# First expert's gating on ScalarE instead of GpSimd, early second x sums, one store a tile, and a new order for the last pair, in an attention and routed-experts kernel

## The chip, the cores and the metric

The kernel runs on one core of one Trainium2 chip. Its time is the device time of one execution, in microseconds (us); the number that counts is the median of three runs. TensorE is called PE, VectorE DVE, ScalarE ACT, GpSimd POOL and SyncE SP, as the profile has them.

## The reference

Two computations follow each other. The first is a linear attention over q, k and v of [8 batches, 8 heads, 576 positions, 64 features]; its result, written as one row for each batch and position, is `x` of [4608, 512]. The second sends every row through eight experts, each a two-layer network, and adds them up with weights that eight rounds of balancing make:

```
phi(t) = concat(relu(t) * cos(theta), relu(t) * sin(theta))
kv  = phi(k)^T v            z = sum over positions of phi(k)
x   = (phi(q) kv) / (phi(q) z + 1e-6)
P   = exp(x @ w_gate - max)                       # [4608, 8]
8 times:  P /= row sums;  P /= column sums;  P *= 4608/8
out = sum over e of P[:, e] * (relu(x @ w1[e]) @ w2[e])
```

`w1[e]` is [512, 1024] and `w2[e]` [1024, 512]. Inputs and output are f32; the kernel multiplies in f16 and adds in f32.

## The kernel before

**Layout.** Rows of `x` are counted in an order of the kernel's own: position p*9+c of batch b is row p of chunk w = 9b+c, 64 rows a chunk. A tile `g` is 128 rows, chunks 2g and 2g+1, so there are 36 tiles. `acc(g)` is the f32 output tile of 128x512 in SBUF (`acc_lo` for the first 32, `acc_hi` for the last four), and `xT` holds `x` transposed in f16.

**Phase 1, to about 230 us.** Attention of one batch after the other is interleaved by a table of slots with expert 0's two layers, in nine blocks of 512 rows. Expert 0's result goes into `acc` without its weight, for the weights are not known yet. Beside the last two blocks run the first steps of the balancing (`balanced`), and the first `x_sums`. In this phase PE, DVE and ACT are reached through `te`, `ve` and `se`, wrappers (`InOrder`) that bind each engine to the written order of instructions. Where `ve` or `se` is set back to the engine itself, a scheduler orders the instructions: in the kernel before, ACT is free from the start of phase 2 and DVE after the first unit of expert 1.

**Phase 2, experts 1 to 7.** Each expert runs six units `n` of 2x384 rows (one half from the first half of the rows and one from the second), about 18.3 us a unit. Both layers use a scheme with seven products in place of eight for a 2x2 block multiplication, which needs sums of inputs beforehand.
- `x_sums` makes three sums of `x` for a unit (S1, S2, S4) and overwrites one part of `xT`, four DVE instructions in all, and saves the three sums in DRAM by three SP transfers; `x_again` loads them back for the later experts. The tiles have two buffers.
- `group` is the first layer of 128 hidden features and their partners: seven products of two matmuls with 384 columns. It uses three PSUM banks, X (`h_ps`), Y (`copied_ps`) and Z (`p7_ps`). ACT copies X to Y (L712), takes the snapshots u2 and u4 (L699) and the two relus of Y and X (L722, L731); DVE closes the two others (`add_relu`, L693). X is written by four products in a row, each after ACT has read the one before.
- After each product of `group` stands a `fill()`. From the second unit on, `pair_fill` puts one step of the second layer there, three times out of four.
- `Pair` is the second layer of one unit's third: two tiles g1 and g2, in seven steps P1, P2, P7, P6, P4, P5, P3 of four matmuls with 256 columns. U and V are the halves of one of three PSUM banks (`rows`), W half a bank more; ACT copies U to W after P1 (L790), DVE makes four sums of the hidden features (`sums`, L774, f16), and DVE adds to `acc` with the expert's weight (`add`, L760). In the very last pair, `sums` runs on POOL, and is written ahead of the steps that are left after the last group. The order of all steps is a list sorted by `OFFSETS` (`OFFSETS_LAST` for the last pair).
- `gate(n)` (L901) multiplies the six expert-0 tiles of unit n by P[:, 0] on POOL, 36 instructions in place, after each unit of expert 1 is written and before its pairs add to those tiles.
- `store` (L163 to L170) writes a finished tile to DRAM by two transfers of 64 rows, both on SP; for the last pair the second one goes through ACT.

POOL also issues the loads of the next expert's weights (L118, L124), written after the gates.

Of the kernel before, what the change touches and what calls it, by code (L numbers as in the profile page):

```python
# [14 lines left out]
ALU = mybir.AluOpType  # L15
# [10 lines left out]
def kernel(  # L26
# [26 lines left out]
    assert KT == HK and N % TCH == 0  # L53
# [109 lines left out]
    def store(g, both=False):  # L163
        for half in range(2):
            w_ = 2 * g + half
            b, c = w_ // C, w_ % C
            rows = out[b * S : (b + 1) * S].rearrange("(p c) d -> p c d", c=C)
            (nc.scalar if half and both else nc.sync).dma_start(
                out=rows[:, c, :], in_=acc(g)[half * HP : (half + 1) * HP, :]
            )  # L170

# [417 lines left out]
    se = nc.scalar  # L589
# [107 lines left out]
    def snapshot(ps, name):  # L697
        t = u_pool.tile([P, TU], F16, name=name)
        nc.scalar.copy(out=t[:], in_=ps[:, 0:TU])  # L699
        return t  # L700
# [3 lines left out]
    def group(hT, tw, xs, n, i, fill):  # L704

        b11, T1, b21, b22, T2, T3, T4 = tw
        s1, s2, s4 = (t[:] for t in xs)
        h11, h12 = hT[:, i, 0:TU], hT[:, FH + i, 0:TU]
        h21, h22 = hT[:, i, TU : 2 * TU], hT[:, FH + i, TU : 2 * TU]
        X = ps_h[0].tile([P, TCH], FP32, name="h_ps")  # L710
        product(X, b11, x_part(0, 0, n), True)
        nc.scalar.copy(out=Y[:, 0:TU], in_=X[:, 0:TU])  # L712
        fill()
        for fn in late:
            fn()
        late.clear()
        fill()
        product(X, T2, s2, False)
        u2 = snapshot(X, "u2")
        fill()  # L720
        product(Y, b21, x_part(0, 1, n), False)
        nc.scalar.activation(out=h11, in_=Y[:, 0:TU], func=AF.Relu)  # L722
        fill()
        product(X, T1, s1, False)
        u4 = snapshot(X, "u4")
        fill()
        product(Z, T3, x_part(1, 0, n), True)
        add_relu(h22, Z, u4)
        fill()
        product(X, b22, s4, False)  # L730
        nc.scalar.activation(out=h12, in_=X[:, 0:TU], func=AF.Relu)  # L731
        fill()

        def last():
            product(Z, T4, x_part(1, 1, n), False)
            add_relu(h21, Z, u2)

        late.append(last)


    class Pair:
        def __init__(self, k, hT, e, w, c1, g1, c2, g2, first, last):
# [5 lines left out]
            self.U, self.V = self.rows[:, 0:DH], self.rows[:, DH : 2 * DH]  # L748
            self.W = W2[:, k % 2 * DH : (k % 2 + 1) * DH]
# [8 lines left out]
        def add(self, g, rows, a=None):  # L758
            a = acc(g) if a is None else a
            ve.scalar_tensor_tensor(  # L760
                out=a, in0=rows, scalar=P_tok[:, g, self.e : self.e + 1], in1=a,
                op0=ALU.mult, op1=ALU.add,
            )

        def sums(self):
# [3 lines left out]
            for out_, in0, in1, op in (  # L769
                (S1[:], self.a21, self.a22, ALU.add), (S2[:], S1[:], self.a11, ALU.subtract),  # L770
                (self.a21, self.a11, self.a21, ALU.subtract),
                (S4[:], self.a12, S2[:], ALU.subtract),
            ):
                (nc.gpsimd if self.last else ve).tensor_tensor(  # L774
                    out=out_, in0=in0, in1=in1, op=op
                )
            self.S1, self.S2, self.S4 = S1[:], S2[:], S4[:]

        def step(self, name):
# [3 lines left out]
            if name == "P1":  # L783
# [6 lines left out]
                nc.scalar.copy(out=self.W, in_=self.U)  # L790
                if not self.last:
                    self.sums()
            elif name == "P7":
# [4 lines left out]
                self.mult(self.V, self.a21, tw2[1])  # L798
            elif name == "P6":
                self.mult(self.U, self.S2, tw2[0])  # L800
                self.add(self.g2, self.rows)
            elif name == "P2":
                self.mult(self.W, self.a12, b21)
                self.add(self.g1, self.W, acc(self.g1)[:, 0:DH])
            elif name == "P4":
                self.mult(self.V, self.a22, tw2[2])
                if self.last:
                    self.add(self.g2, self.V, acc(self.g2)[:, 0:DH])
                    store(self.g2, True)
# [9 lines left out]
            elif name == "P3":  # L819
                self.mult(self.U, self.S4, b22)  # L820
                self.add(self.g1, self.U, acc(self.g1)[:, DH:Dm])
                if self.e == E - 1:
                    store(self.g1, self.last)
# [73 lines left out]
    def gate(n):  # L897

        for pair in of_unit(n):
            for g in pair[::-1]:  # L900
                nc.gpsimd.tensor_scalar(  # L901
                    out=acc(g), in0=acc(g), scalar1=P_tok[:, g, 0:1], scalar2=None, op0=ALU.mult,
                )
# [8 lines left out]
    xs_next = x_tiles()  # L912
    sums_x = x_sums(0, xs_next)
    for j in range(B - 1, NJ):
        hT = next_h()
        tiles = halves(hT, w0, [(ts * P, j * TCH // P + ts) for ts in range(TCH // P)])
        for slot in range(NS):
# [8 lines left out]
            if j == B - 1 and slot:  # L926
                next(sums_x, None)
            since = (j - B + 1) * NS + slot - 5
# [8 lines left out]
    OFFSETS_LAST = {"P1": 0, "P7": 4, "P6": 5, "P2": 7, "P5": 8, "P4": 9, "P3": 10}  # L937
    stream = []
    slot2 = -2
    n_pairs = 0  # L940

    def add_pairs(hT, e, w, n):
        nonlocal n_pairs
        for i, (g1, g2) in enumerate(of_unit(n)):
            last = e == E - 1 and n == NU - 1 and i == UG - 1
            pair = Pair(n_pairs, hT, e, w, i * P, g1, TU + i * P, g2, n == 0 and i == 0, last)
            for name, offset in (OFFSETS_LAST if last else OFFSETS).items():
# [15 lines left out]
    def pair_fill():  # L963
        nonlocal k_fill, slot2
        k_fill += 1
        if k_fill % 4 and stream and stream[0][0] <= slot2:
            _, pair, name = stream.pop(0)
            pair.step(name)
        slot2 += bool(k_fill % 4)

    mark(Y[:])
    for e in range(1, E):
        w = w_next
        for n in range(NU):
            hT = next_h()
            xs = xs_next
            for i in range(FH):
                group(hT, tws[i], xs, n, i, start_fill if e == 1 and n == 0 else pair_fill)
                m = (n + 1) % NU
                if e == 1 and m:  # L980

                    if i == 0:
# [17 lines left out]
            if e == 1 and n == 0:  # L1000
# [6 lines left out]
                w2_first(w)  # L1007
                ve = nc.vector
            if e == 1:
                gate(n)  # L1010
# [8 lines left out]

    stream[-1][1].sums()  # L1020
    while stream:
        _, pair, name = stream.pop(0)
        pair.step(name)
# [28 lines left out]
```

The softmax here doesn't subtract the row's maximum and nothing guards it: scores larger than these inputs give would overflow.

## Time and profile before

| | |
|---|---|
| three runs | 1012.5, 1012.6, 1011.53 us; median 1012.5 |
| the profiled execution's own time | 1011.92 us |
| its span, first to last instruction | 1010.2 us |
| mean granted clock of PE | 0.994 |
| the 36 gates on POOL | 226.7 to 287.4 us, shortest 1.55 us, median 1.57 |
| units of expert 1 (start of the first product) | 231.8, 251.8, 271, 290.5, 308.7 us |
| last unit's second layer begins, span ends | 988.5, 1010.2 us |
| first and last store issued by SP | 906.9, 1006.6 us |
| PE busy in 230 to 327, in 327 to 897, in 897 to 1010.2 | 92.8 of 97, 568.6 of 570, 104.7 of 113.2 us |

The page is one execution. Its first lines give the busy time of each engine, as microseconds, share of the span, and instructions. The slices cut the span in 40 (25.3 us each), with the busy tenths of each engine, one digit a slice. A group line reads: line, engine, operation, output and inputs with shapes, count, then busy microseconds and mean nanoseconds of one, then the idle time just before them and what ended it. A window line gives, for a stretch, its length, then the busy time (and count) of PE, of PE's weight loads, of DVE, ACT and POOL, then the granted clock, the busy share of the 16 DMA engines, and GB/s. A waits line gives who waited for what, and total microseconds, times and the longest. A timeline line gives start, duration, engine, line, operation and tiles, and in brackets the idle time before it and what ended it.

### The profile page before, as it was taken

How to read it: one execution, taken by the hardware profiler on the slowest of the kernel's cores; microseconds unless marked ns; L12 is line 12 of the kernel's file. 1: busy time of each engine (PE TensorE's matmuls, PEld its weight loads, DVE VectorE, ACT ScalarE, POOL GpSimd, SP SyncE). 2: the span in 40 equal slices, each digit the busy share in tenths (PEclk: the TensorE clock that was granted, in tenths of full speed). 3: DMA queues.
4: the chain of work that ended last, by engine and by line, in shares of the span. 5: the costliest groups of instructions: out<-in, count | busy, mean ns of one | idle time of the engine just before them, and what ended most of it. 6: DMA issues, size and time to landing. Idle time of an engine off the chain costs nothing.

```text
span 1010.2 us, 20651 instructions
## 1 busy us (share of the span) xinstructions
PE 983.8 (97%) x8062; PEld 690.7 (68%) x8062; DVE 840.3 (83%) x1861; ACT 556.5 (55%) x1250; POOL 117.3 (12%) x116
## 2 busy tenths in 40 slices
PE   7999999998999999999999999999999999999996
PEld 6555555445677777777777777777777777777775
DVE  5888777689999888888879888988789888987876
ACT  5766666355555555555555555555555555555551
POOL 6312200009930000000000000000000000000001
PEclk8999999999999999999999999999999999999998
DMA  9966510531302331044013310133103401114434
GB/s 168 201 91 86 88 20 1 107 58 41 81 24 50 64 67 47 25 80 76 25 48 66 65 49 25 36 78 66 49 24 67 89 25 33 39 33 127 113 87 113
DMA packets 51762, 66.50 MB, mean 66 GB/s; under 512 B 4816, under 2 KB 43472, under 8 KB 51664
## 3 DMA queue, kind: packets, MB, share of 16 engines
q0 software_dynamic: 27232, 30.94, 19.8%
q1 hardware_dynamic: 24272, 33.98, 12.4%
q8 instruction: 63, 1.03, 0.4%
q14 instruction: 35, 0.29, 0.1%
q10 hardware_dynamic: 160, 0.26, 0.1%
HBM read 83.12 MB, written 12.98 MB: 95 GB/s over the span
## 4 chain that ended last, share of the span: by engine, by line
PE 88%; DVE 9%; DMA 1%; issue 1%; ACT 1%; POOL 0%; DVEq 0%; POOLq 0%; ACTq 0%
PE rows_ps L100 32%; PE h_ps L100 25%; PE p_ps L100 10%; PE copied_ps L100 10%; PE y_ps L100 5%; PE small_ps L100 4%; DVE H L693 1%; DVE k_p L100 1%; DVE acc_lo L760 1%; DMA k_ld<-in_k_dram 1%; DVE q_pT L100 1%; DVE acc_hi L760 1%; DVE q_p L100 0%; DMA q_ld<-in_q_dram 0%; DVE den L100 0%
## 5 line engine op out<-in xcount | busy, mean ns | idle before, releaser
L760 DVE SCALAR_TENSOR_TENSOR acc_lo<-rows_ps,P_tok,acc_lo 128x512 f32<-128x512 f32 (+1 forms) x322 | 205.0, 640 | 75.1 <-PE rows_ps L100 75.1
L100 PEld LDWEIGHTS <-H 128*128 128x128 f16 x2080 | 203.5, 98 | 85.6 <-DVE H L774 2.3
L100 PEld LDWEIGHTS <-w1e 128*128 128x128 f16 x1632 | 155.8, 98 | 58.3 <-issue 3.6
L100 PE MATMUL h_ps<-xT,w1e 128*128 128x384 f16 (+1 forms) x616 | 152.9, 350 | 0.0
L731 ACT ACTIVATE H<-h_ps 128x384 f16<-128x384 f32 x168 | 82.5, 491 | 112.0 <-PE h_ps L100 112.0
L712 ACT COPY copied_ps<-h_ps 128x384 f32<-128x384 f32 x168 | 78.7, 468 | 41.2 <-PE h_ps L100 40.3
L722 ACT ACTIVATE H<-copied_ps 128x384 f16<-128x384 f32 x168 | 82.7, 492 | 23.5 <-PE copied_ps L100 23.5
L100 PE MATMUL rows_ps<-w2e,H 128*128 128x256 f16 (+1 forms) x568 | 91.7, 286 | 0.0
L100 PE MATMUL copied_ps<-xT,w1e 128*128 128x384 f16 x336 | 82.1, 326 | 0.0
L100 PE MATMUL copied_ps<-w2e,H 128*128 128x256 f16 x504 | 75.6, 273 | 0.0
L118 POOL DMA_DIRECT2D w1e<-in_moe_w_dram x11 | 8.3, 770 | 455.2 <-DVE T_3_10517 L671 83.4
L760 DVE SCALAR_TENSOR_TENSOR acc_lo<-copied_ps,P_tok,acc_lo 128x256 f32<-128x256 f32 x126 | 60.1, 477 | 0.5
L760 DVE SCALAR_TENSOR_TENSOR acc_hi<-rows_ps,P_tok,acc_hi 128x512 f32<-128x512 f32 (+1 forms) x57 | 42.0, 736 | 20.5 <-PE rows_ps L100 20.3
L790 ACT COPY copied_ps<-rows_ps 128x256 f32<-128x256 f32 x126 | 45.0, 357 | 23.3 <-PE rows_ps L100 23.0
L901 POOL TENSOR_SCALAR acc_lo<-acc_lo,P_tok 128x512 f32<-128x512 f32 x32 | 53.2, 1678 | 16.7 <-DVE P_tok L100 16.6
L100 PE MATMUL y_ps<-w2e,hT 128*128 128x512 f16 x224 | 54.7, 380 | 0.0
L774 DVE TENSOR_TENSOR H<-H 128x512 f16<-128x512 f16 x125 | 54.1, 433 | 0.0
L100 ACT ACTIVATE hT<-h_ps 128x512 f16<-128x512 f32 x54 | 32.3, 600 | 17.0 <-PE h_ps L100 16.6
L100 DVE TENSOR_TENSOR xT<-small_ps,rb 128x384 f16<-128x384 f32 x64 | 26.2, 451 | 16.6 <-ACT rb L100 16.5
L100 PEld LDWEIGHTS <-hT 128*128 128x128 f16 x224 | 19.5, 98 | 25.0 <-issue 5.8
L100 ACT COPY rb<-small_ps 128x384 f32<-128x384 f32 x64 | 22.4, 402 | 22.7 <-PE small_ps L100 22.6
L100 DVE TENSOR_SCALAR q_pT<-small_ps 128x384 f16<-128x384 f32 x46 | 25.0, 553 | 9.3 <-PE small_ps L100 8.8
(2450 smaller groups left out, 2036.3 us busy)
## 6 DMA issues: line engine op xcount, KB each, us to landing
out_dram<-acc_lo SPq DMA_DIRECT2D x63, 128.0 KB, 2.4
w1e<-in_moe_w_dram POOLq DMA_DIRECT2D x7, 1024.0 KB, 9.0
w2e<-in_moe_w_dram POOLq DMA_DIRECT2D x7, 1024.0 KB, 9.3
k_ld<-in_k_dram POOLq DMA_DIRECT2D x16, 288.0 KB, 6.3
v_ld<-in_v_dram POOLq DMA_DIRECT2D x16, 288.0 KB, 6.9
q_ld<-in_q_dram POOLq DMA_DIRECT2D x16, 288.0 KB, 6.4
w1e<-in_moe_w_dram POOLq DMA_DIRECT2D x4, 256.0 KB, 10.5
w2e<-in_moe_w_dram POOLq DMA_DIRECT2D x4, 256.0 KB, 10.8
```

The costliest lines, as they stand in the source:

```text
L100: i = getattr(self.engine, name)(*args, **kwargs)
L118: nc.gpsimd.dma_start(out=w[0][:, :, f0:f1], in_=view[:, :, f0:f1])
L693: latest = ve._custom_dve(TENSOR_ADD_SAT, out=out, in0=ps[:, 0:TU], in1=t[:], s0=FP32_MAX, s1=0.0)
L712: nc.scalar.copy(out=Y[:, 0:TU], in_=X[:, 0:TU])
L722: nc.scalar.activation(out=h11, in_=Y[:, 0:TU], func=AF.Relu)
L731: nc.scalar.activation(out=h12, in_=X[:, 0:TU], func=AF.Relu)
L760: ve.scalar_tensor_tensor(out=a, in0=rows, scalar=P_tok[:, g, self.e : self.e + 1], in1=a, op0=ALU.mult, op1=ALU.add,)
L774: (nc.gpsimd if self.last else ve).tensor_tensor(out=out_, in0=in0, in1=in1, op=op)
L790: nc.scalar.copy(out=self.W, in_=self.U)
L901: nc.gpsimd.tensor_scalar(out=acc(g), in0=acc(g), scalar1=P_tok[:, g, 0:1], scalar2=None, op0=ALU.mult,)
```

## The change

Five things are changed.

1. **Gates.** `gate` handles one tile. Two of the 36 stay on POOL, written at the end of expert 1's first unit. The others go to ACT (`se.mul` with the weight as a scale for each partition), one after a fill of `group` by a rule on the fill's number, while any are left: 34 gates at six places in 28 fills. ACT keeps the written order through expert 1 and is set free at expert 2.
2. **x sums of unit 1.** They are made beside the last block of phase 1, one DVE instruction a slot, with their three saves, instead of beside unit 0 of expert 1.
3. **Stores.** A tile goes out by one transfer whose DRAM side is [2 chunks, 64 rows, columns], where its two chunks lie in one batch; where they don't (every ninth tile), by two. Stores of half the columns are possible.
4. **The last unit.** The last pair's sums on POOL are written after the first product of the pair before, and wait for that pair's last sum on DVE. In all pairs the second and third of the four sums change places.
5. **The last pair.** V lies in the bank Z, apart from U. P6's add becomes two of half the columns. P2 comes second, and half of g1 is stored after it, the other half after P3; g2 is stored through ACT's queue.

```diff
-    def store(g, both=False):
-        for half in range(2):
-            w_ = 2 * g + half
-            b, c = w_ // C, w_ % C
-            rows = out[b * S : (b + 1) * S].rearrange("(p c) d -> p c d", c=C)
-            (nc.scalar if half and both else nc.sync).dma_start(
-                out=rows[:, c, :], in_=acc(g)[half * HP : (half + 1) * HP, :]
-            )
+    def store(g, cols=slice(0, Dm), queue=nc.sync):
+        w_ = 2 * g
+        b, c = w_ // C, w_ % C
+        rows = out.rearrange("(b p c) d -> b c p d", b=B, c=C)
+        if c + 1 < C:
+            queue.dma_start(
+                out=rows[b, c : c + 2, :, cols],
+                in_=acc(g)[:, cols],
+            )
+        else:
+            queue.dma_start(out=rows[b, c, :, cols], in_=acc(g)[0:HP, cols])
+            queue.dma_start(out=rows[b + 1, 0, :, cols], in_=acc(g)[HP:P, cols])
...
-    se = nc.scalar
...
     def snapshot(ps, name):
         t = u_pool.tile([P, TU], F16, name=name)
-        nc.scalar.copy(out=t[:], in_=ps[:, 0:TU])
+        se.copy(out=t[:], in_=ps[:, 0:TU])
         return t
...
         product(X, b11, x_part(0, 0, n), True)
-        nc.scalar.copy(out=Y[:, 0:TU], in_=X[:, 0:TU])
+        se.copy(out=Y[:, 0:TU], in_=X[:, 0:TU])
         fill()
...
             self.rows = rows2[k % 3][:]
             self.U, self.V = self.rows[:, 0:DH], self.rows[:, DH : 2 * DH]
+            if last:
+                self.V = Z[:, 0:DH]
             self.W = W2[:, k % 2 * DH : (k % 2 + 1) * DH]
 
-        def sums(self):
+        def sums(self, after=None):
             name = "hs_last" if self.last else "hs"
             pool = u_pool if self.last else hs_pool
             S1, S2, S4 = (pool.tile([P, FH, P], F16, name=f"{name}{k_}") for k_ in (1, 2, 4))
             for out_, in0, in1, op in (
-                (S1[:], self.a21, self.a22, ALU.add), (S2[:], S1[:], self.a11, ALU.subtract),
+                (S1[:], self.a21, self.a22, ALU.add),
                 (self.a21, self.a11, self.a21, ALU.subtract),
+                (S2[:], S1[:], self.a11, ALU.subtract),
                 (S4[:], self.a12, S2[:], ALU.subtract),
             ):
-                (nc.gpsimd if self.last else ve).tensor_tensor(
+                i = (nc.gpsimd if self.last else ve).tensor_tensor(
                     out=out_, in0=in0, in1=in1, op=op
                 )
+                if self.last and after is not None:
+                    tc.add_manual_dep(
+                        i.ins,
+                        after.ins.name,
+                        mybir.DependencyInfo(
+                            mybir.DependencyClass.Sync, mybir.DependencyReason.DATA
+                        ),
+                        reason="VectorE's sums first",
+                    )
+                    after = None
+            self.summed = i
             self.S1, self.S2, self.S4 = S1[:], S2[:], S4[:]
 
         def step(self, name):
...
                 self.mult(self.U, self.a11, b11, True)
-                nc.scalar.copy(out=self.W, in_=self.U)
+                se.copy(out=self.W, in_=self.U)
                 if not self.last:
                     self.sums()
             elif name == "P7":
...
-                self.mult(self.V, self.a21, tw2[1])
+                self.mult(self.V, self.a21, tw2[1], self.last)
             elif name == "P6":
                 self.mult(self.U, self.S2, tw2[0])
-                self.add(self.g2, self.rows)
+                if self.last:
+                    self.add(self.g2, self.U, acc(self.g2)[:, 0:DH])
+                    self.add(self.g2, self.V, acc(self.g2)[:, DH:Dm])
+                else:
+                    self.add(self.g2, self.rows)
             elif name == "P2":
                 self.mult(self.W, self.a12, b21)
                 self.add(self.g1, self.W, acc(self.g1)[:, 0:DH])
+                if self.last:
+                    store(self.g1, slice(0, DH))
             elif name == "P4":
                 self.mult(self.V, self.a22, tw2[2])
                 if self.last:
                     self.add(self.g2, self.V, acc(self.g2)[:, 0:DH])
-                    store(self.g2, True)
+                    store(self.g2, queue=nc.scalar)
             elif name == "P5":
                 self.mult(self.U, self.S1, b12)
                 if self.last:
...
                 self.mult(self.U, self.S4, b22)
                 self.add(self.g1, self.U, acc(self.g1)[:, DH:Dm])
                 if self.e == E - 1:
-                    store(self.g1, self.last)
+                    store(self.g1, slice(DH if self.last else 0, Dm))
 
     tw2 = [None] * 3
 
...
 
         return [(n * UG + i, NG // 2 + n * UG + i) for i in range(UG)]
 
-    def gate(n):
-
-        for pair in of_unit(n):
-            for g in pair[::-1]:
-                nc.gpsimd.tensor_scalar(
-                    out=acc(g), in0=acc(g), scalar1=P_tok[:, g, 0:1], scalar2=None, op0=ALU.mult,
-                )
+    def gate(g, pool=None):
+
+        if pool is None:
+            se.mul(out=acc(g), in_=acc(g), mul=P_tok[:, g, 0:1])
+        else:
+            pool.tensor_scalar(
+                out=acc(g), in0=acc(g), scalar1=P_tok[:, g, 0:1], scalar2=None, op0=ALU.mult,
+            )
+
+    ungated = [g for n in range(NU) for pair in of_unit(n) for g in pair]
 
 
     balance = sinkhorn()
...
     for i in range(FH):
         tw, tw_steps[3 + i] = w1_steps(w_next, i)
         tws.append(tw)
-    xs_next = x_tiles()
+    xs_first = [x_tiles() for _ in range(2)]
+    xs_next = xs_first[0]
     sums_x = x_sums(0, xs_next)
     for j in range(B - 1, NJ):
         hT = next_h()
...
                 gates(B - 1, Z[:])
             if j == B - 1 and slot:
                 next(sums_x, None)
+            if j == NJ - 1:
+                if slot == 0:
+                    sums_x = x_sums(1, xs_first[1])
+                next(sums_x, None)
             since = (j - B + 1) * NS + slot - 5
             if since == -4:
                 balanced(3)
...
     OFFSETS = {"P1": 0, "P2": 3, "P7": 4, "P6": 5, "P4": 8, "P5": 9, "P3": 13}
 
-    OFFSETS_LAST = {"P1": 0, "P7": 4, "P6": 5, "P2": 7, "P5": 8, "P4": 9, "P3": 10}
+    OFFSETS_LAST = {"P1": 0, "P2": 3, "P7": 4, "P6": 7, "P5": 8, "P4": 9, "P3": 10}
     stream = []
+    final = []
     slot2 = -2
     n_pairs = 0
 
...
         for i, (g1, g2) in enumerate(of_unit(n)):
             last = e == E - 1 and n == NU - 1 and i == UG - 1
             pair = Pair(n_pairs, hT, e, w, i * P, g1, TU + i * P, g2, n == 0 and i == 0, last)
+            if e == E - 1 and n == NU - 1:
+                final.append(pair)
             for name, offset in (OFFSETS_LAST if last else OFFSETS).items():
                 stream.append((7 * n_pairs + offset, pair, name))
             n_pairs += 1
...
         if k_fill % 4 and stream and stream[0][0] <= slot2:
             _, pair, name = stream.pop(0)
             pair.step(name)
+        if (k_fill % 7 == 6 or k_fill % 7 == 4 and k_fill % 4 in (1, 2)) and ungated:
+
+            gate(ungated.pop(0))
         slot2 += bool(k_fill % 4)
 
     mark(Y[:])
     for e in range(1, E):
+        if e == 2:
+            se = nc.scalar
         w = w_next
         for n in range(NU):
             hT = next_h()
...
                 m = (n + 1) % NU
                 if e == 1 and m:
 
+                    if n == 0:
+                        xs_next = xs_first[1]
+                        continue
                     if i == 0:
                         xs_next = x_tiles()
                         sums_x = x_sums(m, xs_next)
...
                     pass
                 mark(W2[:])
                 w2_first(w)
+                for _ in range(2):
+                    gate(ungated.pop(0), nc.gpsimd)
                 ve = nc.vector
-            if e == 1:
-                gate(n)
             if n == 0 and e + 1 < E:
                 w_next = new_weights(wA if e % 2 else wB)
                 load_w1(w_next, e + 1, 1)
...
             add_pairs(hT, e, w, n)
     for fn in late:
         fn()
-
-    stream[-1][1].sums()
     while stream:
         _, pair, name = stream.pop(0)
         pair.step(name)
+        if pair is final[-2] and name == "P1":
+
+            final[-1].sums(pair.summed)
```

## The prediction

> **What bounds the kernel now.** I read the page's busy times and slices first, then busy time by stretch, what TensorE (PE) waits for, the order of time in two places, and the transfers.
>
> ```profile
> span 1010.2 us, 20651 instructions
> PE 983.8 (97%) x8062; PEld 690.7 (68%) x8062; DVE 840.3 (83%) x1861; ACT 556.5 (55%) x1250; POOL 117.3 (12%) x116
> ...
> POOL 6312200009930000000000000000000000000001
> ...
> L901 POOL TENSOR_SCALAR acc_lo<-acc_lo,P_tok 128x512 f32<-128x512 f32 x32 | 53.2, 1678 | 16.7 <-DVE P_tok L100 16.6
> ```
>
> PE is busy 97% of the span, so only its pauses can be won. POOL works in two places late on: the gates (L901), and the very end. Busy time by stretch (PE first, granted clock after POOL) shows what goes with that:
>
> ```profile
> 245.00:250.00 5.00, 3.86 (x31) 2.81 (x29) 4.43 (x9) 2.09 (x5) 5.00 (x4) 1.00 0.11 39
> ...
> 290.00:295.00 5.00, 5.00 (x41) 3.80 (x39) 5.00 (x12) 2.83 (x7) 0.00 (x0) 1.00 0.24 84
> ```
>
> With POOL gating, PE loses 1.14 us of five; without it, and with the same x sums on VectorE (DVE), nothing. PE's waits from 229 to 290:
>
> ```profile
> PE p_ps L100 <- DVE H L693: 3.5, 5, 1.1
> PE h_ps L100 <- ACT u_3843 L699: 0.3, 1, 0.3
> PE h_ps L100 <- ACT copied_ps L712: 0.3, 1, 0.3
> ```
>
> From 290 to 327, still in expert 1, the same view has no line. The end in order of time:
>
> ```profile
> 991.18 1.37 DVE L774 TENSOR_TENSOR H<-H 128x512 f16<-128x512 f16 x1
> ...
> 992.60 0.61 PE L100 MATMUL rows_ps<-V_12078,H 128*128 128x256 f16 x4 [1.98 <-DVE H L774]
> ...
> 994.55 0.99 PE L100 MATMUL rows_ps<-w2e,hs_13178 128*128 128x256 f16 x4 [0.90 <-DVE acc_hi L760]
> ...
> 1006.00 0.48 DVE L760 SCALAR_TENSOR_TENSOR acc_lo<-rows_ps,P_tok,acc_lo 128x256 f32<-128x256 f32 x1 [0.69 <-PE rows_ps L100]
> 1006.55 0.47 SPq L168 DMA_DIRECT2D out_dram<-acc_lo  x1
> ```
>
> DVE's sums take 1.3 to 1.4 us beside POOL's and 0.42 alone (971.4 to 973). PE pauses 2.9 us, and its next groups of four come 0.85 us apart instead of 0.44, at a granted clock of 0.70 (995 to 1000).
>
> The profiled execution took 1011.92 us: the span and 1.7 around it. The median of three is 1012.5, 0.6 above it. I sum on the span, then add 2.3.
>
> **Gates off POOL.** 34 of 36 gates (1.55 us each) leave POOL, two stay at the start. The 3.5 us of PE's waits on DVE go, as in 290 to 327: -3.5 (bounds -2.5 and -3.9). The three waits on ScalarE (ACT), 0.8 us with one of 0.2, stay.
>
> **Gates on ACT.** An ACT copy of 128x512 f32 out of PSUM takes 586 ns. Nothing here shows it from SBUF with a scale per partition; nearest are the two sines of 128x576 from SBUF, 667 ns, and 774 with a bias tile. Less 64 elements (53 ns by the copies' slope) that is 0.61 to 0.72; I take 0.72, the tile operand being there too. Consecutive ACT instructions overlap by 0.1, so a gate occupies 0.62. Behind it waits the next PSUM read, and behind that PE, which reuses the bank. Per unit of 28 fills the rule gates at fills 6, 13, 18, 20, 25, 27. At 6, 20, 25 and 27 ACT has the room (idle 0.6 to 1.0 before L731; at 25 PE does another step first). At 13 a pair's copy (L790, 297.72 to 298.08 in the unit from 290) stands ahead of the gate: h12 (L731) moves from 298.05 to 298.60, the copy of X behind it (L712) from 298.87 to 298.99, and PE's next product on X from 299.38 to 299.50: 0.12. At 18:
>
> ```profile
> 282.30 0.49 ACT L722 ACTIVATE H<-copied_ps 128x384 f16<-128x384 f32 x1 [0.28 <-PE copied_ps L100]
> ...
> 283.06 0.48 ACT L699 CAST u_4407<-h_ps 128x384 f16<-128x384 f32 x1 [0.27 <-PE h_ps L100]
> ...
> 283.62 0.49 PE L100 MATMUL h_ps<-S_4087,w1e 128*128 128x384 f16 x2
> ```
>
> The gate runs 282.69 to 283.41, u4 ends at 283.79 instead of 283.54, and the product starts at 283.84 instead of 283.62: 0.22. So 6 units x 0.34 = +2.0 (0.8 with the cheap gate; at most 21, if none of the 34 x 0.62 hid). The adds that wait for a gate come eight fills later or more (some 5 us): nothing. POOL's weight loads (L118, L124) stood behind the gates; they come sooner and are wanted an expert later: nothing. ACT's written order in expert 1 is the order it has now: nothing.
>
> **Second x sums early.** Four DVE sums (0.55, 0.47 apart) and three stores (0.32 of SP each, which has nothing else then) leave 215 to 231 for 200 to 207. Three of the old places were idle time of DVE (at 215.9 and 221.8 it waited for PE); the fourth, at 230.8, is in the 3.5. In the new place one fits the idle 0.6 us at 201.6; the other three stand before the reciprocal at 205.95, which ends near 207.05 while PE asks for it at 206.81: +0.24 (0 to 0.5).
>
> **The tail.** Call the last unit's pairs a, b and c and the pair before them z. POOL's four sums for c now wait for b's last DVE sum; nothing else is queued on POOL, and c's P7, P6, P5 and P3 wait for them. Rebuilt from a's first sum at 989.41, with DVE sums of 0.42 (0.34 apart), the trace's adds (0.48 for 256 columns, 0.75 for 512) and products 0.44 apart: a's P7 at 990.46, z's P3 at 991.65, c's P1 at 995.69, POOL's sums 994.6 to 999.3 (1.15 each; the trace has 1.15 to 1.33), c's P6 at 998.6. Then U and V lie in two banks, so P4 no longer waits for P5's add: P5 999.76, P4 1000.2, P3 1000.92, last add to 1002.03, store at 1002.1 instead of 1006.55: -4.45. P6's add becomes two of 0.48 for one of 0.75, and P2's half store one more issue on SP, both counted in this or beside it. Half a tile in the last store: -0.6 (0 to -1). Reordering the other pairs' sums costs nothing: P7 comes earlier. Sum -5.0 (-3.5 to -6).
>
> **One store a tile.** Two issues of 0.55 us become one; SP waits anyway. But the transfer's form changes. Each old store walks 64 rows of DRAM. The new one walks 2 chunks of 64 rows against 128 partitions; no transfer in the trace has an outermost count under 64, so none shows how two are shared out. Bounds: as now (128 KB lands in 2.4 us), or one engine to each outer index, two in all. Then an engine moves 64 rows of 2 KB a tile. Single packets of the stores took 84 ns (quickest twentieth) to 151 (median, when all 16 read one half of the partitions); two engines alone are nearest to 84: 5.4 us a tile, where a tile comes each 3.05 us (six in 18.3). 32 of 36 tiles have this form: 32 x 64 x 0.084 = 172 us on each of the two engines, against 99 us from first store to last. I take this end: the sharing must follow some count in the pattern, and the outer one is the only one here that differs from all the transfers seen spread.
>
> The Trainium skill's "DMA: Bandwidth & Descriptors" ("Why a DMA increments its semaphore by 16 and not by 1") speaks against the change: the engines used are the largest number up to 16 that divides the slowest count of both patterns, here two. By this rule the sum is the 172 us; by its advice, in the same page's rules, to use one 128-partition transfer for two halves it would be nothing.
>
> **Sum.** Up to the first store: -3.5 + 2.0 + 0.2 = -1.3, so that it is issued at 905.7. Then 0.5 + 172, the nine x loads on the same engines (9 x 8 rows x 0.07 = 5), the split tiles (3), and 1.3 from the last packet to the end (it was near 1008.9): 1087.5. With 2.3 around it: **1090**. The x loads, wanted some 20 us after issue, are met by a backlog of 14 to 22: their stall hides in this. At 75 to 95 ns a packet: 1070 to 1112; at 151, 1227.
>
> **Rivals.**
> 1. Stores spread as now: -1.3 - 5.0 = -6.3, span 1003.9, time **1006** (1002 to 1010). For it: every transfer in the trace is spread, and the waits it removes are plain. Against it: the untried form.
> 2. Stores spread, but gates hide badly: ACT is in PE's loop, one PSUM read after another. From 9.3 us of stalls (0.25 for each of 34) it is slower than before by 1; with all 21 unhidden, 1025. Against it: ACT is 55% busy, with 112 us idle before L731.
> 3. DVE, 85% busy, stalls PE without POOL too: only the tail is won, 1009. Against it: 290 to 327. It counts as faster.
>
> **How the numbers follow.** Forecast 0.55; rivals 1 and 3 together 0.40; rival 2 0.05, of which 0.03 lands within 0.2% (2 us, about what a measurement can tell). So slower 0.57, same 0.03, faster 0.40. The range goes from rival 1's low end to 1110, about 95 ns a packet; dearer packets (0.12) are left out. The forecast's own range is 1070 to 1110.
>
> **What would show it.** Right: after the last add (near 1002) nothing but DMA for some 80 us, a DMA share near 2/16 in that stretch, landings far over 2.4 us. For the rest in either case: PE's waits on DVE H gone from 229 to 290, new waits on u4 of some 0.2 in every second to third group of expert 1, the clock at 1.00 from 990 to 1000, DVE's sums at 0.42 there. Wrong: landings of 2 to 4 us for 256 KB.

## The result, and the profile after

The changed kernel takes 1081.0 us (median of four runs, 1080.5 to 1082.0) where the kernel before took 1012.0 beside it: a ratio of 1.068 (95% interval 1.066 to 1.070). The forecast was 1090, its own range 1070 to 1110. The profiled execution took 1080.8 us, its span is 1079.1.

The page of the changed kernel, cut to its span, busy times, the slices of PE's clock and of the DMA engines, and the queue that SP issues on:

```profile
span 1079.1 us, 20593 instructions
PE 985.2 (91%) x8062; PEld 690.9 (64%) x8062; DVE 830.4 (77%) x1862; ACT 574.9 (53%) x1284; POOL 60.3 (6%) x82
...
PEclk8999999999999999999999999999999999998755
DMA  9956400731013310331033103310331101221121
...
DMA packets 50932, 66.49 MB, mean 62 GB/s; under 512 B 3858, under 2 KB 42770, under 8 KB 50834
...
q1 hardware_dynamic: 23472, 33.97, 10.1%
```

PE does the same work (985 us against 984) in a span 69 us longer. The same slices of the kernel before:

```profile
DMA  9966510531302331044013310133103401114434
```

There the last four slices, with the stores, read 3 and 4; now the store phase reads 1 and 2. Busy time by stretch shows the end (after the length: PE, its weight loads, DVE, ACT, POOL, then granted clock, DMA share, GB/s):

```profile
990.00:995.00 5.00, 5.00 (x40) 3.62 (x38) 3.45 (x7) 1.93 (x5) 0.00 (x0) 1.00 0.13 50
995.00:1000.00 5.00, 4.65 (x43) 4.01 (x42) 4.93 (x13) 0.62 (x2) 0.00 (x0) 1.00 0.13 52
...
1020.00:1079.00 59.00, 0.00 (x0) 0.00 (x0) 0.00 (x0) 0.00 (x0) 0.00 (x0) 0.50 0.16 57
```

From 1020 on no engine computes. A DMA share of 0.13 is two of sixteen engines. The 0.16 of the last stretch takes in the transfers of two split tiles, which SP issues up to 1029; from 1040 to 1075 the share is 0.13 again. SP's queue and the last add in order of time (start, duration, engine):

```profile
902.66 4.07 SPq L168 DMA_DIRECT2D out_dram<-acc_lo  x2
...
933.25 7.12 SPq L658 DMA_DIRECT2D S_12635<-x_saved  x1
...
958.83 4.92 SPq L658 DMA_DIRECT2D S_12863<-x_saved  x1
...
969.77 52.45 SPq L168 DMA_DIRECT2D out_dram<-acc_lo  x11
...
1007.52 0.48 DVE L766 SCALAR_TENSOR_TENSOR acc_lo<-rows_ps,P_tok,acc_lo 128x256 f32<-128x256 f32 x1 [0.25 <-PE rows_ps L100]
...
1054.30 13.40 SPq L168 DMA_DIRECT2D out_dram<-acc_lo  x3
```

SP needs 4.8 us an issue on average (52.45 for 11) where one took half a microsecond: it stands in front of a queue that drains no faster. The loads of the x sums (L658) stand in the same queue. What PE waits for, from 229 to 290 and then from 897 to 985:

```profile
PE h_ps L100 <- ACT u_3839 L100: 0.3, 1, 0.3
PE h_ps L100 <- ACT copied_ps L100: 0.3, 1, 0.3
PE h_ps L100 <- ACT u_3792 L100: 0.2, 1, 0.2
...
PE h_ps L100 <- DMA S_12863<-x_saved: 5.1, 1, 5.1
PE h_ps L100 <- DMA S_12635<-x_saved: 1.3, 1, 1.3
PE h_ps L100 <- DMA S_12864<-x_saved: 0.8, 1, 0.8
```

The waits on DVE H beside the gates are gone, and 7.2 us of waits on loads are new. In the wait of 5.1 the granted clock falls to half, from 971.3 to 978.1 (6.8 us, the last 1.4 of the wait among them), and the matmul groups of four take 1.06 instead of 0.60.

One note on the numbers below. The first `add_relu` starts at 213.8 us in the profile of before and between 213.3 and 215.3 in the others, ahead of nearly all edits. So where single profiles are compared, times are counted from there to the last add (before: 792.7 us); the verdicts rest on the medians of runs.

### The profile page after: what moved, and what is told of

Its sections match the earlier page's. It is cut to its first block, busy times and chain, and to the rows that moved or that the text cites. A ratio compares the mean times of both kernels' runs of the same rounds, so it can differ in the third digit from the quotient of the medians.

```text
span 1079.1 us, 20593 instructions
## 1 busy us (share of the span) xinstructions
PE 985.2 (91%) x8062; PEld 690.9 (64%) x8062; DVE 830.4 (77%) x1862; ACT 574.9 (53%) x1284; POOL 60.3 (6%) x82
## 4 chain that ended last, share of the span: by engine, by line
PE 66%; issue 20%; DVE 4%; ACT 1%; DMA 1%; POOL 1%; POOLq 0%; ACTq 0%; DVEq 0%
PE rows_ps L100 23%; PE h_ps L100 19%; PE copied_ps L100 8%; PE p_ps L100 7%; PE y_ps L100 5%; PE small_ps L100 4%; DVE k_p L100 1%; DMA v_ld<-in_v_dram 1%; DVE q_pT L100 1%; DVE q_p L100 0%; DMA q_ld<-in_q_dram 0%; DVE den L100 0%; DVE acc_lo L100 0%; DVE P_tok L100 0%; DVE v_aug_240 L100 0%
## 5 line engine op out<-in xcount | busy, mean ns | idle before, releaser
L734 ACT ACTIVATE H<-h_ps 128x384 f16<-128x384 f32 x144 | 70.6, 490 | 97.3 <-PE h_ps L100 97.3
L715 ACT COPY copied_ps<-h_ps 128x384 f32<-128x384 f32 x144 | 67.5, 469 | 35.3 <-PE h_ps L100 35.3
L725 ACT ACTIVATE H<-copied_ps 128x384 f16<-128x384 f32 x144 | 70.8, 492 | 20.7 <-PE copied_ps L100 20.7
L808 ACT COPY copied_ps<-rows_ps 128x256 f32<-128x256 f32 x111 | 39.7, 357 | 17.9 <-PE rows_ps L100 17.9
L100 ACT ACTIVATE H<-h_ps 128x384 f16<-128x384 f32 (+1 forms) x40 | 21.3, 532 | 15.4 <-PE h_ps L100 14.7
```

What stands on the lines that cost most here:

```text
L100: i = getattr(self.engine, name)(*args, **kwargs)
L715: se.copy(out=Y[:, 0:TU], in_=X[:, 0:TU])
L725: se.activation(out=h11, in_=Y[:, 0:TU], func=AF.Relu)
L734: se.activation(out=h12, in_=X[:, 0:TU], func=AF.Relu)
L808: se.copy(out=self.W, in_=self.U)
```

## Experiments: the stores

**Two transfers a tile again, all else as changed.**

```diff
-        if c + 1 < C:
-            queue.dma_start(out=rows[b, c : c + 2, :, cols], in_=acc(g)[:, cols])
-        else:
-            ...
+        b2, c2 = (w_ + 1) // C, (w_ + 1) % C
+        queue.dma_start(out=rows[b, c, :, cols], in_=acc(g)[0:HP, cols])
+        queue.dma_start(out=rows[b2, c2, :, cols], in_=acc(g)[HP:P, cols])
```

> The changed kernel with every tile stored by two transfers of 64 rows again (the halves of columns, the queues and all else of the change kept). Theory A (the store's form alone makes it slow): in the trace of the changed kernel the work of expert 7 is 4.57 us ahead of before at 946 us, ahead of the first stall on a load, and gains 4.2 us more from there to the last add; without the 7.2 us of stalls on the x loads and the slower clock behind them the whole gain shows: 1011.6 - 4.6 - 4.2 = 1002.8, 1001.5 to 1004.5 with the last store. Theory B (the sum of the prediction as it stands): 1006. Theory C (gates or the new tail carry a part of the loss): over 1012. DMA share of the store phase back to over 0.3 in A and B.

Measured: 1004.2 us, ratio to before 0.9925 (0.9912 to 0.9937). The store's form alone makes the change slow; without it the change is 7.6 us faster than before by the ratio. The time is at the upper end of theory A's range, below theory B. The DMA share of the store phase is back where it was before (0.45 and 0.38 in the same two stretches):

```profile
903.00:953.00 50.00, 50.00 (x386) 37.48 (x384) 41.12 (x90) 27.87 (x63) 0.00 (x0) 1.00 0.47 121
953.00:985.00 32.00, 32.00 (x247) 23.90 (x246) 25.54 (x55) 17.44 (x39) 0.00 (x0) 1.00 0.40 91
```

**Only one store a tile, in the kernel before.**

```diff
+        b, c = 2 * g // C, 2 * g % C
+        if c + 1 < C:
+            rows = out.rearrange("(b p c) d -> b c p d", b=B, c=C)
+            nc.sync.dma_start(out=rows[b, c : c + 2, :, :], in_=acc(g))
+            return
```

> The kernel before, with nothing changed but one transfer for each of the 32 tiles whose two chunks lie in one batch. Theory A (two DMA engines share a transfer whose outermost count is 2): the backlog starts with the first store at 906.9 and takes what it took in the changed kernel, 175 us from first store to last packet, then 1.3 to the end and 1.8 around the span: 1085, 1080 to 1090, with 2 closing writes for each such store. Rival (one transfer a tile costs nothing by itself, the loss is the change's other parts): 1012.

Measured: 1084.4 us, ratio 1.0715 (1.0700 to 1.0729), 0.6 from theory A. The page's line on packets, of the kernel before and of this one:

```profile
DMA packets 51762, 66.50 MB, mean 66 GB/s; under 512 B 4816, under 2 KB 43472, under 8 KB 51664
```

```profile
DMA packets 50802, 66.49 MB, mean 61 GB/s; under 512 B 3856, under 2 KB 42512, under 8 KB 50704
```

There are 960 small packets fewer, which is 32 stores x 30: two transfers closed by 16 small writes each have become one closed by two. With the DMA share of 0.13 this shows two engines to a store.

**The 64 rows written as 4 x 16.**

```diff
+        rows = out.rearrange("(b q r c) d -> b c q r d", b=B, q=4, c=C)
+        queue.dma_start(out=rows[b, c, :, :, cols], in_=acc(g)[0:HP, cols])
```

> As the kernel with two transfers of 64 rows a tile, but each transfer's DRAM side is written as [4, 16, columns] in place of [64, columns]: the same bytes to the same places. Theory A (the outermost count sets how many engines share a transfer): 4 closing writes for each store in place of 16, four engines with 32 rows x 0.084 = 2.7 us a tile against the 3.05 us in which a tile comes, so that they keep up, but the last stores land later and the x loads too: 1003 to 1010, DMA share near 4/16. Rival (what is slow is that one transfer takes 128 partitions or two chunks at once, or the four and 16 are merged into 64 on the way): the same time as with [64, columns], within 0.5, and 16 closing writes.

Measured: 1003.8 us, ratio 0.9920 (0.9905 to 0.9935), and 4848 small packets, as many as with [64, columns]. The 4 and the 16 follow each other without a gap in the address and, by this count of packets, were merged on the way, so this says nothing on a count of four; it is a second measurement of the kernel with two transfers. That the *outermost count* sets the share is thus shown for 64 (sixteen engines) and 2 (two engines) alone. One transfer a tile with the rows ahead of the chunks was not tried, so it is not shown that a single transfer of 128 partitions would be quick in another form.

**Ten stores of the new form.** Only the whole tiles of units 0 and 1 of expert 7 go out by one transfer.

```diff
-        if c + 1 < C:
+        if c + 1 < C and g % (NG // 2) < 6:
```

> The changed kernel with one transfer for the ten whole tiles of units 0 and 1 of expert 7, and two transfers of 64 rows for every other tile. Theory A (the two engines' backlog costs only what of it is left at the end, or what holds up a load): ten tiles put 54 us on the two engines within the first 37 us of stores; with the others' share of some 0.6 a tile the backlog is gone near 970, 30 us before the end: 1004 to 1006, the upper end if a load of x is late. Theory B (every such store costs its share of the loss, 77 us over 32): 1004 + 24 = 1028.

Measured: 1004.7 us, ratio 0.9931 (0.9917 to 0.9944): 0.5 to 0.9 more than with none, which is within the intervals. Busy time by stretch:

```profile
903.00:953.00 50.00, 48.65 (x373) 36.21 (x372) 39.83 (x87) 26.82 (x62) 0.00 (x0) 1.00 0.24 79
953.00:985.00 32.00, 32.00 (x247) 23.91 (x245) 25.53 (x56) 17.60 (x40) 0.00 (x0) 1.00 0.62 154
```

The backlog builds up to 953 (share 0.24, one wait of 1.4 us on a load of x) and is made good by 985 (0.62). A slow transfer costs what of it is left at the end, plus what it holds up in its queue.

**Expert 7's x loads on ACT's queue,** in the changed kernel as it is.

```diff
-            nc.sync.dma_start(
+            (nc.scalar if last_e else nc.sync).dma_start(
                 out=t[:].rearrange("p k t -> p (k t)"), in_=x_saved[n, i]
```

> The changed kernel as it is, one store a tile, but expert 7's loads of the x sums go through ACT's queue instead of SP's, so that no load stands behind the stores in a queue. Theory A (the prediction: PE's stalls on these loads lie inside the stores' backlog and cost nothing by themselves): PE's 7.2 us of waits on x_saved gone or under 1 us, the last add near 998 instead of 1008, and the time the same as the changed kernel's within 1.5: 1079.5 to 1082. Theory B (the stalls are on the path to the end): 10 less, 1071.

Measured: 1081.5 us, ratio 1.0689 (1.0674 to 1.0704). The last add ends at 1003.4 instead of 1008.0, and the time doesn't move: the stalls lie inside the backlog, as the prediction had it. They didn't go as far as expected. What PE waits for, then what ACT waits for:

```profile
PE h_ps L100 <- ACT u L704: 4.1, 1, 4.1
```

```profile
ACT u L704 <- DMA out_dram<-acc_lo: 5.8, 2, 5.2
```

ACT's snapshot stood behind ACT's own load, whose issue was held up: the trace names a store's landing as what ended it. That this load, spread over all engines, waited for the two that the stores filled is the plain reading; no run separates it.

## Experiments: the other parts, each alone

**Gates alone, in the kernel before** (the change's `gate`, its rule for the fills, and ACT's written order through expert 1).

```diff
+        if (k_fill % 7 == 6 or k_fill % 7 == 4 and k_fill % 4 in (1, 2)) and ungated:
+            gate(ungated.pop(0))
...
-            if e == 1:
-                gate(n)
```

> The kernel before with the gates alone moved: 34 of 36 on ACT after a fill, by the change's rule, two left on POOL; ACT keeps the written order through expert 1. Theory A (from the two traces: the changed kernel goes from 0.63 behind to 2.4 ahead between the start of expert 1 and its end, x sums early included): 3.0 faster, 1008.6. Theory B (the prediction's two terms, -3.5 and +2.0): 1.5 faster, 1010.1. Theory C (gates stall ACT's reads of PSUM in earnest): no gain or slower, 1012 to 1025, with PE waits on u and copied_ps of ACT.

Measured: 1008.8 us, ratio 0.9967 (0.9956 to 0.9978): 3.3 faster, theory A. In the profile it is 2.8 ahead of before at the last `add_relu`, and 1.1 more at the last add, where PE's clock stays at 1.00 behind the same pause of 2.0. The stretch behind that pause, first before, then here:

```profile
995.00:1000.00 5.00, 5.00 (x34) 3.86 (x33) 4.13 (x9) 0.36 (x1) 0.00 (x0) 0.70 0.48 108
```

```profile
990.00:995.00 5.00, 3.32 (x28) 2.64 (x28) 4.97 (x9) 0.36 (x1) 1.72 (x2) 1.00 0.27 61
```

So some 1.1 us of this part's gain comes with the clock; why it stayed up here is not shown.

**Early x sums alone.**

```diff
+            if j == NJ - 1:
+                if slot == 0:
+                    sums_x = x_sums(1, xs_first[1])
+                next(sums_x, None)
```

> The kernel before, with unit 1's x sums alone moved beside the last block of phase 1. Theory A (the trace of the changed kernel: 0.22 lost at the reciprocal near 207, 0.40 given back between 230 and 232, where the fourth sum stood): 1011.9 to 1012.4, no change that can be measured. Theory B (the prediction's term, +0.24 and nothing back): 1012.5. Theory C (it also makes part of what the changed kernel wins in experts 2 to 7): 1010.5 or less.

Measured: 1012.05 us, ratio 1.0001 (0.9992 to 1.0010): nothing.

**The order of a pair's sums alone.**

```diff
-                (S1[:], ...), (S2[:], S1[:], self.a11, ALU.subtract),
-                (self.a21, self.a11, self.a21, ALU.subtract),
+                (S1[:], ...), (self.a21, self.a11, self.a21, ALU.subtract),
+                (S2[:], S1[:], self.a11, ALU.subtract),
```

> The kernel before, with only the second and third of a pair's four sums exchanged. In the two traces the changed kernel wins 0.3 at the turn from unit 0 to unit 1 of every expert from 2 on, 2.2 in all, which the gates alone don't bring. Theory A (the new order of the sums brings it: P7 finds its operand one sum sooner): 1010.2, and PE's five waits of 0.2 on DVE H between 327 and 897 gone. Theory B (the prediction: the order of the sums costs and brings nothing): 1012.3.

Measured: 1006.4 us, ratio 0.9949 (0.9936 to 0.9961): 5.2 faster by the ratio, the largest gain of any part, and more than either theory gave. PE's waits on DVE H from 229 to 897, one line each from before, the gates alone and the order alone:

```profile
PE p_ps L100 <- DVE H L693: 4.7, 10, 1.1
```

```profile
PE p_ps L100 <- DVE H L692: 1.5, 6, 0.3
```

```profile
PE p_ps L100 <- DVE H L693: 1.5, 5, 0.4
```

With both (two transfers a tile) there is no such line. And in the tail of the order alone, in order of time:

```profile
985.05 0.56 DVE L775 TENSOR_TENSOR hs<-H 128x512 f16<-128x512 f16 x1
...
985.64 1.26 DVE L775 TENSOR_TENSOR H<-H 128x512 f16<-128x512 f16 x1
...
986.96 0.61 PE L100 MATMUL rows_ps<-V,H 128*128 128x256 f16 x4 [0.69 <-DVE H L775]
```

P7 reads the sum that is now the second instead of the third. POOL still slows DVE's sums (1.26 for 0.42), but PE waits 0.69 here and 0.68 for the next one, instead of 1.98, and the granted clock stays at 1.00 where it was 0.70 before.

Where the gain comes from can be counted in the profile: the lead over before is 1.7 us at 327, at the end of expert 1, 3.9 at the last `add_relu` and 5.6 at the last add. So some 2.2 us are won in experts 2 to 7, of which the view of waits names 1.5 (six waits on DVE H); the rest is not explained.

**The tail alone** (POOL's sums behind DVE's, V in its own bank, the last pair's new order, halves of g1's columns; two transfers a tile, other pairs' sums as before).

```diff
+        if pair is final[-2] and name == "P1":
+            final[-1].sums(pair.summed)
...
+            if last:
+                self.V = Z[:, 0:DH]
```

> The kernel before with the last unit of the change alone: the last pair's sums on POOL wait for DVE's, V lies in its own bank, the last pair's order is the new one, g1 goes out by halves of the columns; two transfers of 64 rows a tile, all else as before. Theory A (the trace of the kernel with two transfers and all else: it is 3.7 ahead at the last add_relu and its span is 7.1 shorter, so the tail alone brings 3.4): 1008.9. Theory B (the prediction's sum for the tail): 5.0 faster, 1007.3. Theory C (POOL's sums, now 4 x 1.15 behind DVE's, end too late, and P6 waits as long as P7 did): 1011 or more.

Measured: 1008.0 us, ratio 0.9966 (0.9953 to 0.9978): 3.4 faster by the ratio, as A had it, and 4.1 by the medians, between A and B. The last add comes 4.4 sooner (788.3 after the first `add_relu`, for 792.7), but the way from it to the end of the span grows from 3.7 to 5.1:

```profile
1002.52 0.48 DVE L761 SCALAR_TENSOR_TENSOR acc_lo<-rows_ps,P_tok,acc_lo 128x256 f32<-128x256 f32 x1 [0.24 <-PE rows_ps L100]
...
1003.42 0.60 SPq L169 DMA_DIRECT2D out_dram<-acc_lo  x1
1004.11 0.55 SPq L168 DMA_DIRECT2D out_dram<-acc_lo  x1
1004.71 0.59 SPq L169 DMA_DIRECT2D out_dram<-acc_lo  x1
```

The last half tile is ready at 1003.0 and issued at 1004.1 and 1004.7: SP is still busy with the issues of the tiles before it. (This profile is the slowest of the five runs. In the six others that have the new tail and end with two transfers a tile, the same way is 4.0 to 4.6.)

**Two transfers a tile and the old order of the sums.**

```diff
                 (S1[:], self.a21, self.a22, ALU.add),
-                (self.a21, self.a11, self.a21, ALU.subtract),
                 (S2[:], S1[:], self.a11, ALU.subtract),
+                (self.a21, self.a11, self.a21, ALU.subtract),
```

> The changed kernel with two transfers of 64 rows a tile, and the four sums of a pair in the order of before. Theory A (the order by itself wins 0.3 at the turn of each expert from 2 on and shares the rest of its 5.6 with the gates and the tail, which cure the same waits): 2.0 to 2.5 slower than with the new order, 1006.2 to 1006.7, which is what the prediction's sum gave. Theory B (the order's gain is all its own): 5.6 slower, 1009.6. Theory C (the gates and the tail cure it all): 1004.0.

Measured: 1005.4 us, ratio 0.9938 (0.9924 to 0.9951), 1.2 more than with the new order by the medians, 2.2 by the profiles (785.5 to the last add for 783.3). Theory B is out: most of the order's 5.2 is a gain that the gates and the tail make too. What it adds to them is some 1 to 2 us; the intervals of the two kernels overlap, so the size is not sharp. By the profiles the difference is made in experts 2 to 7, and PE's waits from 229 to 897 name a part of it: five of 0.2, one an expert, which the new order takes away.

```profile
PE p_ps L100 <- DVE H L691: 1.2, 5, 0.2
```

**The gates at other fills, two transfers a tile.**

```diff
-        if (k_fill % 7 == 6 or k_fill % 7 == 4 and k_fill % 4 in (1, 2)) and ungated:
+        if k_fill % 28 in (1, 6, 20, 22, 25, 27) and ungated:
```

> The changed kernel with two transfers a tile, and the gates at fills 1, 6, 20, 22, 25 and 27 of a unit's 28 instead of 6, 13, 18, 20, 25 and 27. Theory A (only the gates at 13 and 18 cost: in expert 1 the products behind them come 0.16 and 0.21 late, 0.37 a unit, and the idle time of ACT ahead of u2 at fills 1 and 22, 0.73 and 0.98, covers a gate of 0.62): 5 to 6 units x 0.37 = 1.9 to 2.2 faster than with the change's places, 1002. Theory B (the gates cost wherever they stand, since ACT's reads and PE's products take turns): as with the change's places, 1004. Theory C (a gate ahead of u2 delays it in most groups): slower, 1005 or more.

Measured: 1002.15 us, ratio 0.9908 (0.9894 to 0.9921), 2.0 less than with the change's places by the medians (1.6 less than the run with 4 x 16), 1.4 by the profiles (781.9 for 783.3). The change's places first (from the run with 4 x 16), then the new ones, around the two fills of one unit:

```profile
294.81 0.72 ACT L100 ACTIVATE acc_lo<-acc_lo,P_tok 128x512 f32<-128x512 f32 x1
295.43 0.48 ACT L100 ACTIVATE H<-h_ps 128x384 f16<-128x384 f32 x1
...
295.10 0.49 PE L100 MATMUL h_ps<-xT,w1e 128*128 128x384 f16 x2
...
296.34 0.48 PE L100 MATMUL h_ps<-S,T 128*128 128x384 f16 x2
...
297.86 0.49 PE L100 MATMUL h_ps<-S,w1e 128*128 128x384 f16 x2
...
299.15 0.48 PE L100 MATMUL h_ps<-S,w1e 128*128 128x384 f16 x2
```

```profile
293.78 0.49 PE L100 MATMUL h_ps<-xT,w1e 128*128 128x384 f16 x2
...
294.87 0.48 PE L100 MATMUL h_ps<-S,T 128*128 128x384 f16 x2
...
296.39 0.49 PE L100 MATMUL h_ps<-S,w1e 128*128 128x384 f16 x2
...
297.48 0.49 PE L100 MATMUL h_ps<-S,w1e 128*128 128x384 f16 x2
```

Two products on X lie 1.24 and 1.29 apart with a gate at fills 13 and 18, and 1.09 both times without: 0.15 and 0.20 a unit. The view of waits shows neither. Nothing that was run is faster.

**P4 ahead of P5 in the last pair, on top of that** (g2's store stands behind P5 then).

```diff
-    OFFSETS_LAST = {"P1": 0, "P2": 3, "P7": 4, "P6": 7, "P5": 8, "P4": 9, "P3": 10}
+    OFFSETS_LAST = {"P1": 0, "P2": 3, "P7": 4, "P6": 7, "P4": 8, "P5": 9, "P3": 10}
```

> The kernel with two transfers a tile and the gates at fills 1, 6, 20, 22, 25 and 27, and in the last pair P4 ahead of P5, g2's store behind P5. Theory A (P5 waits 0.57 for the add that reads U; P4 reads and writes the other bank and can stand in between): 0.4 faster than with P5 first, 1001.7. Theory B (the last add is bound by POOL's fourth sum, which ends at the same time): 1002.15.

Measured: 1002.4 us, ratio 0.9908 (0.9894 to 0.9921): no gain, and not for theory B's reason. The wait has moved. P5 waited 0.57 for the add that reads U; now P3, which writes U next, waits 0.57 for P5's add:

```profile
995.62 0.60 PE L100 MATMUL rows_ps<-w2e,hs_last 128*128 128x256 f16 x4 [0.57 <-DVE acc_hi L761]
```

## Why the prediction was right, step by step

**The store's form was the step that decided, and it held.** Two engines for a transfer whose outermost count is 2: the share of 0.13, two closing writes, and the kernel before with this edit alone at 1084.4 show it. No row of the trace before had decided between the two ends of this term; the prediction chose by an argument, with a chance of 0.55. The Trainium skill's rule ("DMA: Bandwidth & Descriptors", "Why a DMA increments its semaphore by 16 and not by 1") agrees with the runs at both counts that they had, 64 and 2. The advice that the prediction set beside this rule, one transfer of 128 partitions for two halves, is the wrong one for this form: the one transfer cost 72 us in the kernel before.

One sign that was named could not be read: the view of transfers gives these stores no landing time.

**The size.** The sum gave a span of 1087.5; it is 1079.1. The first store came at 902.66, not 905.7 (-3.0): the gates and the sums' order, mis-sized below, come ahead of it. From there to the end the prediction had 181.8 us and the trace has 176.4. A packet of 2 KB does take 84 ns in the records, but they overlap a little: from 980 to 1020 each of the two engines moves 496.5 packets in 40 us, one in 80.6 ns. So 32 x 64 x 0.0806 = 165 in place of 172 (-7); the first packet came 1.3 after the issue instead of 0.5. With the terms for x loads and split tiles as they were (5 and 3, neither measured singly) and 1.3 at the end the sum is 175.6, 0.8 short.

**The stall on the x loads** was foreseen as hidden in the backlog, and the run with these loads on ACT's queue shows it: the last add moved by 4.6 us, the time by 0.6 the other way. Not foreseen was that SP itself is held at each issue, for 4.8 us.

**Gates off POOL, -3.5, and on ACT, +2.0.** The sum of the two, -1.5, was mis-sized: alone they bring 3.3. The price on ACT was right to the place (0.12 and 0.22 forecast, 0.15 and 0.20 measured), though what moving these two gates brought in the profiles is 1.4 and not 2.0. The gain was too small. It was taken from the waits view, which lists what it can name. Counted from the first `add_relu`, the kernel with the gates alone is 3.1 ahead by 290 us, where the last gate on POOL would be over, with some 1.1 of the price paid (3.2 units x 0.35), so the gates' leaving POOL is worth some 4.2, an estimate from these numbers; up to 327 it gives back 0.7.

**"Reordering the other pairs' sums costs nothing."** This is the step that failed. By itself the order is worth 5.2 us. The prediction had named the mechanism (P7 comes earlier) and priced it at nothing, without a reason from a row. The lines of the tail that it showed held the price: P7 there waits 1.98 us for the third sum.

**The tail, -5.0.** The last add's -4.45 is measured at 4.4 in the run with the tail alone. The last store's -0.6 had the wrong sign: +1.4 there, +0.3 to +0.9 in the six other profiles, with two transfers a tile on SP. In the changed kernel neither counts, under the backlog.

**x sums early, +0.24.** In the changed kernel the product that waits for the reciprocal comes 0.22 later than in before, counted against the same shift at 201; near 231, where the fourth sum stood, 0.40 is given back. With the x sums alone the 0.23 is lost too, and nothing comes back near 231 (0.02), where the next sum of x takes 1.02 us instead of 0.55. Both nets are too small for the runs to tell.

**The parts don't add up.** Gates -3.3, order -5.2, tail -3.4 and x sums nothing make -11.9; together they bring 7.6 and 8.1 in the two measurements of that kernel, all by the ratios. Two pauses are cured twice: the waits on DVE H, most of them beside POOL's gates (4.7 us; 1.5 left after either cure, none after both), and P7's wait in the tail. And the half clock of before's tail, some 1.1 us, is missing in the profiles of all three. Rival 1, which was the sum with stores spread as now, said 1006 and is 1004.

**Rival 2** (gates hide badly) needed 9.3 us of stalls on ACT; what was found is about 0.35 a unit. **Rival 3** (DVE stalls PE anyway) holds for little: with the gates alone 1.5 us of waits on DVE H stay, most of them five of 0.2 after 327, and they vanish with the new order.

## What to carry to other kernels

Merging two DMAs into one can change how many engines carry it. Before doing so, look at the outermost count of both sides, and in the profile at the DMA share (2 of 16 is 0.13) and at how long the issuing queue stays on one issue. When an engine waits for one of several results that another makes in a row, put that result first: it cost nothing here and was worth as much as moving 34 instructions to another engine, or more. Measure parts alone and together, since two cures of the same pause count once.

## What the runs showed of the hardware

- A transfer on two engines moves 256 KB in 5.2 us here (64 rows x 80.6 ns), spread over 16 engines 128 KB lands in 2.4.
- The issuing engine was held while the stores' two engines were behind: SP for 4.8 us an issue, and ACT, with loads of its own in a second queue, once for 5.2.
- PE's clock. In a pause of 5.1 us the granted clock fell to half, for 6.8 us. The pause of 2.0 in the tail was followed by 3.4 us at half clock in the kernel before (with one more pause of 0.9 between) and in the one with early x sums, and by none in the one with the gates alone, which has the same two pauses as before. The Trainium skill ("TensorE: Matmul & The Clock Gate", "What's actually happening") tells of a free-running window of 3413 ns in which activity is counted; lengths of 3.4 and 6.8 us agree with it. Why pauses shorter than a window count, and the same ones not another time, is not shown: no run here varied where they fall.
- An ACT multiplication of 128x512 f32 in SBUF by a scale for each partition takes 0.72 us, the upper of the two ends that were forecast.
